# Attention's opening with head 0's scores and values ahead of head 1's maxima, later rotations, and conversions spread over more slots

## The chip, the cores and the metric

The kernel runs on one core of a Trainium2 chip. The metric is the device time of one execution in microseconds; the time before is 953.85 us, the median of three runs (952.25 to 954.91).

## The reference

Four batches of 8 heads of attention (576 positions, 64 dimensions) with rotary embedding of q and k, then a gated feed-forward block that mixes positions, then a low-rank mixing with a two-layer block. Cut to what matters here:

```python
q_rot, k_rot = rotate(q), rotate(k)
scores = q_rot @ k_rot.T / sqrt(64)
scores = scores - max(scores, axis=-1)
attn = exp(scores); attn = attn / (sum(attn, axis=-1) + 1e-9)
x = attn @ v                      # all heads side by side
x = x + gated(x) @ w_out          # gelu, norm, mixing of positions
u = x + (x.T @ U @ V).T
out = u + relu(u @ w_ch1) @ w_ch2
```

## The kernel before

The first phase is attention over 32 heads; the later phases are not touched. Each head is worked in five chunks of 128 positions (the fifth has 64), two halves of 288 columns each. The loop over t from -20 to 162 at the end of attention is the clock of the phase: t counts slots, and a slot is one chunk of one head, five to a head. In each slot TensorE gets one tile of scores (`scores`, tile st, L249), some tiles of maxima (`row_max`, tile sm, L220), and the values (`values`, tile pv, L276) of the chunk three slots back (LAG). Everything else is put in a table by `later(t, fn)` and issued at the end of its slot. The order on every engine is the order in which this loop issues; all engines are scheduled by hand here, and each works its own queue in order.

Precision is kept by splitting a number into a rounded high part and the low part that is left. For each head the kernel builds four stacks of 128 partitions: Q1 and K1 for the first product (high parts, and K's low part below), Q2 and K2 for the second (Q's low part, and one extra row). The extra row of Q2 holds the row maxima, the extra row of K2 is -1, so that the second product also subtracts the maximum. So scores of a head need that head's maxima for all 576 positions: five sm tiles, each reduced by VectorE (tile MX, L225), a transposition on TensorE and a row into Q2. For heads from 2 on the row goes through a 5x128 transpose (L223), a copy (L228) and a DMA on ScalarE's queue (L230); for head 0 `first_row` does it with five products with the identity (L236) and two copies (L237, L238).

The stacks: `load` brings raw q and k (tile raw, 576 KB) over SP's queue, `rope` rotates them in three operations (L148, L149, L150; head 0 on VectorE, head 1 on VectorE and GpSimd, the rest on GpSimd). Heads 0 to 2 are split by `first_stacks` on ScalarE and VectorE (copies L196 and L198, low parts L209 and L210). Later heads go the usual way in `stacks`: `high` is one copy on ScalarE (Q1, L162) and a DMA into K (L164); `low` is a subtraction on GpSimd (L167) and two DMAs (L168 into K1, L169 within Q1). SP issues all of these in order with the raw loads and the rest.

The slots of these steps are tables of numbers. A head from 5 on rotates 26, 25 and 23 slots ahead of its first scores, its high step stands 20 ahead and its low step 17 (LEAD); heads 2 to 4 have LEAD_IN, heads 0 and 1 FIRST. Maxima run up to 13 slots ahead of scores (AHEAD, RAMP): their tiles pass through the three PSUM buffers ss that scores use too, so each needs the reduction or the exponential (L252 on ScalarE) of an earlier one. The values of a head gather in the single buffer pv and are read out by ScalarE (L292).

Two more things stand in the slots. Weights come as 64-bit floats and are converted in chunks on ScalarE, VectorE (four operations, L73 to L76) and GpSimd (MATRIX, SMALL: first slot and distance of steps). From slot 100 the result of the first batch is split again (XH on ScalarE, XL on GpSimd, L426; ROWS). And IDLE places warm matmuls (L439) of a zero tile on TensorE at chosen points of the opening; their result is not used.

```python
upto = 0 if t < -9 else NC if t < MAX_1 else max(2 * NC, min(t + AHEAD + 1, 2 * NC + RAMP * (t - RAMP_FROM) // 10, NC * NH))
```

This line sets how many maxima tiles have been issued by slot t; head 1's five (upto from 5 to 10) go at slot -1, in front of the first scores at slot 0.

Of the kernel before, what the change touches and what calls it, by code (L numbers as in the profile page):

```python
# [53 lines left out]
def tile_kernel(ctx: ExitStack, tc: tile.TileContext, qk, vv, tabs, w_in, g_ln, wsgT, b_sg, w_out, u_r, v_r, w1, w2, out):  # L54
# [98 lines left out]
    def stacks(h, ticks):  # L153
# [16 lines left out]
        if h < len(BY_ACT):  # L170
            steps = rope(nc.gpsimd, h) + first_stacks(h)
        else:
            steps = rope(nc.gpsimd, h) + (high, low)
            if h < NS:
                steps += lambda: nc.gpsimd.memset(f(K2[D:]), -1.0),
            value_stacks(h)
# [11 lines left out]
    def first_stacks(h):
# [4 lines left out]

        def copy(on_act, out, x):
            if on_act:
                nc.scalar.activation(out, x, AF.Copy)  # L196
            else:
                nc.vector.tensor_copy(out, x)  # L198

        def high():  # L200
            e = BY_ACT[h]
            copy(e[0], K1[z], rot[z])
            copy(e[1], K1[a], rot[z])
            copy(e[2], Q1[a], rot[a])
            copy(e[3], Q1[z], rot[a])
            copy(e[4], K2[a], rot[z])

        def low():
            nc.vector.tensor_tensor(K1[z], rot[z], f(K1[z]), ALU.subtract)  # L209
            nc.vector.tensor_tensor(Q2[a, :S], rot[a], f(Q1[a]), ALU.subtract)  # L210
        value_stacks(h)
        return high, low
# [177 lines left out]
    for h in range(1, NR):  # L390
        load(h)
    for i in range(2):
        load_v(i)
    for i in range(len(BY_ACT)):
# [48 lines left out]
    for t in range(T0, NC * NH + LAG):  # L443
# [3 lines left out]
        if 0 <= t < NC * NH:  # L447
            if t < 3:
                warm(7 + t)
# [472 lines left out]
```

## Time and profile before

| | us |
|---|---|
| median of three runs | 953.85 |
| the profiled execution, its own time | 953.18 |
| its span, first to last instruction | 951.4 |
| attention, from the span's start to the next phase's first matmul | 304.95 |
| of it, from the start to the first scores | 32.34 |

| engine | busy, share of the span |
|---|---|
| PE, TensorE's matmuls | 97% |
| DVE, VectorE | 56% |
| ACT, ScalarE | 36% |
| POOL, GpSimd | 39% |

The profile names engines as in the second table; PEld is TensorE's loading of weights, SPq and ACTq are queues that issue DMAs. Shares over the whole span mix phases with different limits, so the stretches and the engines' rows in order of time are read for the phase that the change touches. A busy TensorE counts pipelined matmuls, and the warm matmuls too.

### The profile page before, as it was taken

How to read it: one execution, taken by the hardware profiler on the slowest of the kernel's cores; microseconds unless marked ns; L12 is line 12 of the kernel's file. 1: busy time of each engine (PE TensorE's matmuls, PEld its weight loads, DVE VectorE, ACT ScalarE, POOL GpSimd, SP SyncE). 2: the span in 40 equal slices, each digit the busy share in tenths (PEclk: the TensorE clock that was granted, in tenths of full speed). 3: DMA queues.
4: the chain of work that ended last, by engine and by line, in shares of the span. 5: the costliest groups of instructions: out<-in, count | busy, mean ns of one | idle time of the engine just before them, and what ended most of it. 6: DMA issues, size and time to landing. Idle time of an engine off the chain costs nothing.

```text
span 951.4 us, 13147 instructions
## 1 busy us (share of the span) xinstructions
PE 926.0 (97%) x5180; PEld 786.5 (83%) x5180; DVE 535.3 (56%) x720; ACT 345.6 (36%) x550; POOL 371.2 (39%) x289
## 2 busy tenths in 40 slices
PE   6899999999999998999999899999999999999998
PEld 2588888888877988999999787888888888888887
DVE  7797888887895496334248746642652552222222
ACT  4376656666665543314224323311320320101000
POOL 7788776877741765231427523200210220000000
PEclk7999999999999999999999999999999999999999
DMA  5579767676651500000003002220220210000112
GB/s 176 142 214 189 201 177 194 173 188 177 171 147 27 176 1 1 1 1 23 1 23 112 23 22 62 94 66 1 89 89 1 67 45 0 1 1 23 45 49 85
DMA packets 57300, 77.93 MB, mean 82 GB/s; under 512 B 29755, under 2 KB 33110, under 8 KB 57238
## 3 DMA queue, kind: packets, MB, share of 16 engines
q1 hardware_dynamic: 56928, 77.01, 29.3%
q8 instruction: 41, 0.67, 0.3%
q14 instruction: 21, 0.17, 0.1%
q10 hardware_dynamic: 310, 0.08, 0.0%
HBM read 55.02 MB, written 4.79 MB: 63 GB/s over the span
## 4 chain that ended last, share of the span: by engine, by line
PE 84%; DVE 9%; issue 2%; DMA 2%; POOL 2%; ACT 1%; SPq 0%; DVEq 0%; ACTq 0%; POOLq 0%
PE a L549 21%; PE r L549 20%; PE pv L276 14%; PE st L249 9%; PE w L549 5%; PE sm L220 4%; PE v L549 3%; PE m L549 3%; PE u L549 3%; DVE g L630 1%; DVE t L75 1%; DVE MX L225 1%; DVE t L73 1%; PE t L653 1%; DVE t L76 1%
## 5 line engine op out<-in xcount | busy, mean ns | idle before, releaser
L276 PE MATMUL pv<-pc,VV 128*65 128x288 f32 x512 | 144.7, 405 | 0.5 <-DVE sums L297 0.5
L225 DVE TENSOR_REDUCE MX<-sm 128x1 f32<-128x576 f32 (+1 forms) x160 | 119.1, 752 | 41.1 <-PE sm L220 37.7
L249 PE MATMUL st<-Q,K 65*128 65x288 f32 (+3 forms) x640 | 125.6, 319 | 0.3 <-DVE MX L225 0.3
L742 DVE SCALAR_TENSOR_TENSOR RL<-r,RH 128x1024 fp32r<-128x1024 f32 (+1 forms) x38 | 42.3, 1112 | 123.8 <-ACT RH L741 123.7
L741 ACT ACTIVATE RH<-r 128x1024 fp32r<-128x1024 f32 (+1 forms) x38 | 35.5, 936 | 207.2 <-PE r L549 207.2
L249 PEld LDWEIGHTS st<-Q,K 65*128 65x128 f32 (+3 forms) x640 | 95.9, 179 | 11.8 <-DVE MX L225 1.0
L757 DVE TENSOR_TENSOR X<-a,X 128x256 f32<-128x256 f32 (+4 forms) x65 | 46.4, 745 | 90.8 <-PE a L549 90.7
L252 ACT ACTIVATE pc<-st 128x576 f32<-128x576 f32 x128 | 82.6, 646 | 37.8 <-PE st L249 34.7
L549 PE MATMUL a<-RH,setB 128*128 128x512 f32 (+1 forms) x320 | 93.3, 368 | 0.0
L276 PEld LDWEIGHTS pv<-pc,VV 128*65 128x65 f32 x512 | 68.6, 136 | 29.5 <-DVE sums L297 0.7
L220 PE MATMUL sm<-K,Q 128*128 128x288 f32 (+1 forms) x320 | 76.5, 324 | 11.7 <-ACT K L196 5.8
L549 PE MATMUL a<-RH,setA 128*128 128x512 f32 (+1 forms) x288 | 83.5, 366 | 0.0
L549 PE MATMUL r<-UH,setB 128*128 128x512 f32 (+1 forms) x256 | 73.2, 363 | 0.0
L549 PE MATMUL r<-UH,setA 128*128 128x512 f32 (+1 forms) x256 | 72.9, 363 | 0.1
L220 PEld LDWEIGHTS sm<-K,Q 128*128 128x128 f32 (+1 forms) x320 | 52.3, 184 | 19.6 <-ACT K L196 8.3
L549 PEld LDWEIGHTS a<-RH,setB 128*128 128x128 f32 x320 | 58.2, 188 | 10.0
L513 POOL TENSOR_TENSOR setB<-t,setB 128x512 fp32r<-128x512 f32 x16 | 20.7, 1294 | 102.9 <-ACT setB L702 91.8
L549 PEld LDWEIGHTS a<-RH,setA 128*128 128x128 f32 x288 | 52.1, 188 | 9.2
L549 PE MATMUL a<-RL,setB 128*128 128x512 f32 (+1 forms) x160 | 58.9, 368 | 0.0
L167 POOL TENSOR_TENSOR Q<-raw,Q 128x576 fp32r<-128x576 f32 x29 | 43.0, 1483 | 34.0 <-ACT Q L162 33.9
L149 POOL TENSOR_TENSOR raw<-raw,tab 128x576 f32<-128x576 f32 x31 | 53.8, 1734 | 5.9 <-DMA raw<-in_qk 5.9
L549 PEld LDWEIGHTS r<-UH,setA 128*128 128x128 f32 x256 | 46.1, 188 | 8.4 <-DVE X L683 0.4
(170 smaller groups left out, 1968.4 us busy)
## 6 DMA issues: line engine op xcount, KB each, us to landing
raw<-in_qk SPq DMA_DIRECT2D x31, 576.0 KB
raw<-in_w SPq DMA_DIRECT2D x24, 512.0 KB
K<-Q SPq DMA_DIRECT2D x29, 288.0 KB
VV<-in_vv SPq DMA_DIRECT2D x16, 320.0 KB
rb<-rr SPq DMA_DIRECT2D x15, 288.0 KB
K<-Q SPq DMA_DIRECT2D x29, 144.0 KB
Q<-Q SPq DMA_DIRECT2D x29, 144.0 KB
raw<-in_w_in SPq DMA_DIRECT2D x8, 512.0 KB
```

What stands on the lines that cost most here:

```text
L149: lambda: e.tensor_tensor(raw[:, 1], raw[:, 1], tab[:, 1], ALU.mult),
L167: nc.gpsimd.tensor_tensor(Q2[:, :S], rot, f(Q1), ALU.subtract)
L220: nc.tensor.matmul(ps[:TS[t], n, :HALF], Q1[:, t * P:t * P + TS[t]], K1[:, n * HALF:(n + 1) * HALF], start=True, stop=True)
L225: nc.vector.tensor_reduce(MXs[h % 2][:TS[t], t:t + 1], ps[:TS[t], :, :HALF], AX.XY, ALU.max)
L249: nc.tensor.matmul(ps[:kk, n, :HALF], l[:, c * P:c * P + kk], r[:, ns], start=st, stop=not st)
L252: nc.scalar.activation(h2(pc[:kk]), ps[:kk, :, :HALF], AF.Exp, scale=0.125)
L276: nc.tensor.matmul(o, l, r, start=(c == 0 and j == 0), stop=(c == NC - 1 and j == len(pr) - 1))
L513: return nc.gpsimd.tensor_tensor(out, a, b, ALU.subtract)
L549: nc.tensor.matmul(o, l, rr, start=(j == 0), stop=(j == n - 1))
L741: nc.scalar.activation(RH[:, s], ps[:, :, :WIDE[blk]], AF.Relu)
L742: nc.vector.scalar_tensor_tensor(RL[:, s], ps[:, :, :WIDE[blk]], 0.0, f(RH[:, s]), ALU.max, ALU.subtract)
L757: nc.vector.tensor_tensor(X[b][:, e2, xs], ps[:, :n, us], X[b][:, e2, xs], ALU.add)
```

## The change

The opening is written anew. Head 0: `early_stacks` deals its copies and low parts to ScalarE and VectorE without going through slots; `first_head` issues its five maxima tiles with the row pieces in between, in the pv buffer. Then four scores tiles and three values tiles of head 0 come ahead of head 1's maxima, which are issued in slot 4 around the rest of the values; head 1's row is made the way of head 0's (`row_piece`, tile second_row). Head 1 is rotated on GpSimd alone, behind a memset that waits for one on VectorE, and that one stands behind head 0's low parts. Head 2 takes the usual way over GpSimd and DMAs. Of 39 warm matmuls 26 are left, all at the start.

From head 2 on the slots are: rotation at b, b + 2 and b + 3, high step at high_at(h), low step one slot later, where b is high_at(h - 1) and high_at(h) is the larger of 5h - 20 and 8 + 4.55(h - 4): the second up to head 20, equal or the first from then on. Heads 2 to 4 have numbers of their own (LEADS). Maxima follow `maxima(t)`, which starts 9 slots ahead of scores at slot 12 and comes to 13. SMALL and MATRIX move the conversions; the last five chunks stay at slots 130 to 150. XL's four operations move from slots 134 to 146 to slots 148 to 157. SP's first loads have the first values in front of head 3's raw data.

```diff
-LEAD = 26, 25, 23, 20, 17
-LEAD_IN = (-20, -19, -19, -8, -8), (-19, -18, -16, -3, -1, 4), (-3, -3, 0, 2, 4, 8)
-FIRST = (-17, -10), (-9, -9)
-LOAD, LOAD_V, SPLIT_V = 30, 7, (2, -1)
-AHEAD, RAMP_FROM, RAMP, MAX_1, ROW, ROW_0, ROW_1 = 12, -1, 25, -1, 2, -8, -9
+LEADS = {2: (-8, -8, -8, 3, 3), 3: (-7, 4, 4, 4, 5), 4: (4, 6, 7, 8, 9)}
+LOADS = {4: -6, 5: 3, 6: 5, 7: 7}
+MAXIMA = {5: 12, 6: 14, 7: 15, 8: 15, 9: 17, 10: 19, 11: 20}
+def high_at(h):
+    return max(5 * h - 20, 8 + 455 * (h - 4) // 100)
+def maxima(t):
+    return MAXIMA.get(t) or min(21 + (t - 12) * 25 // 23, t + 13)
+LOAD, LOAD_V, SPLIT_V = 35, 7, (2, -1)
+ROW = 1
-MATRIX = ((20, 1), (40, 10), (80, 10)) + tuple((t, 1) for t in range(130, 155, 5))
-SMALL, CONVERT, ROWS = ((5, 1), (10, 1), (15, 1)), 5, (100, 134)
-IDLE = 17, 2, 5, 0, 2, 5, 6, 1, 0, 1
+MATRIX = ((50, 10), (55, 10), (95, 10)) + tuple((t, 1) for t in range(130, 155, 5))
+SMALL, CONVERT, ROWS = ((5, 5), (25, 5), (90, 10)), 5, (100, 148)
+IDLE = 26
...
+    def early_stacks(h):
...
+        if h == 0:
+            return [act(K1[z], rot[z]), dve(K1[a], rot[z]), dve(Q1[a], rot[a]), act(Q1[z], rot[a])] + lows + [act(K2[a], rot[z])]
+        return [act(K1[a], rot[z]), act(Q1[a], rot[a]), dve(K1[z], rot[z])] + lows + [act(Q1[z], rot[a]), act(K2[a], rot[z])]
...
-            later(tick + 1, lambda: nc.scalar.dma_start(row, f(mt)))
+            if done > 5:
+                later(tick + 1, lambda: nc.scalar.dma_start(row, f(mt)))
+            else:
+                nc.scalar.dma_start(row, f(mt))
+    def row_piece(h, ps, t):
+        nc.tensor.matmul(ps[:1, t // 4, t % 4 * P:(t % 4 + 1) * P], MXs[h][:, t:t + 1], ident, start=True, stop=True)
...
+    def first_head():
+        ps = psp.tile([P, 2, 512], F32, tag="pv", name="first_row", bufs=1)
         for t in range(NC):
-            nc.tensor.matmul(ps[:1, t // 4, t % 4 * P:(t % 4 + 1) * P], MXs[0][:, t:t + 1], ident, start=True, stop=True)
-        nc.scalar.activation(Q2s[0][D:D + 1, :4 * P], ps[:1, 0, :4 * P], AF.Copy)
-        nc.vector.tensor_copy(Q2s[0][D:D + 1, 4 * P:], ps[:1, 1, :P])
+            row_max(0, t, None, 0)
+            if t > 1:
+                row_piece(0, ps, t - 2)
+        for t in (NC - 2, NC - 1):
+            row_piece(0, ps, t)
...
+    load(1)
+    load(2)
+    load_v(0)
+    load(3)
+    load_v(1)
...
+    for fn in rope(nc.vector, 0) + tuple(early_stacks(0)):
         fn()
...
+    nc.vector.memset(MXs[1], 0.0)
+    nc.gpsimd.memset(MXs[1], 0.0)
+    for fn in rope(nc.gpsimd, 1):
+        fn()
+    for tick, fn in zip((-8, -8, -8, -8, -8, 1, 3), early_stacks(1)):
+        later(tick, fn)
+    value_stacks(0)
...
     for h in range(2, NH):
-        stacks(h, LEAD_IN[h - 2] if h < 5 else [NC * h - o for o in LEAD])
+        b = high_at(h - 1)
+        stacks(h, LEADS.get(h) or (b, b + 2, b + 3, high_at(h), high_at(h) + 1))
     for h in range(NR, NH):
-        later(NC * h - LOAD - NC * (h > 2 * NR), lambda h=h: load(h))
+        later(LOADS.get(h) or max(NC * h - LOAD, high_at(h - NR) + 2), lambda h=h: load(h))
...
+        if t == -9:
+            first_head()
+        if t == NC:
+            values(0, 4, t)
+            ps = psp.tile([P, 2, 512], F32, tag="ss", name="second_row", bufs=3)
+            for c in range(NC):
+                row_piece(1, ps, c)
...
         if 0 <= t < NC * NH:
             scores(*divmod(t, NC))
+        if t == NC - 1:
+            for c in range(1, 3):
+                values(0, c, t)
+            for c in range(3):
+                row_max(1, c, None, t)
+            low_parts(len(lows))
+            values(0, 3, t)
+            for c in range(3, NC):
+                row_max(1, c, None, t)
-        upto = 0 if t < -9 else NC if t < MAX_1 else max(2 * NC, min(t + AHEAD + 1, 2 * NC + RAMP * (t - RAMP_FROM) // 10, NC * NH))
+        upto = 0 if t < NC else min(maxima(t), NC * NH)
...
-                    last[m] = t + ROW if m > 1 else ROW_1 if m else ROW_0
+                    last[m] = t + ROW + (m > 12)
...
+        if t == LAG:
+            values(0, 0, t)
```

On TensorE, where head 0's scores begin. Names: sm0_4 is the last maxima tile of head 0, sm1_4 that of head 1, st0_0 the first scores tile, pv0 the values of head 0, pc0_0 its exponentials; the last number only tells buffers apart. Before:

```order
L220 MATMUL sm1_4_288<-K_1_100,Q1_1_95 64x288 x2
L439 LDWEIGHTS idle_117
L439 MATMUL warm_296<-idle_117 128x512
L249 MATMUL st0_0_298<-Q1_0_94,K_0_99 128x288 x2
L249 MATMUL st0_0_298<-Q2_0_104,K_0_99 128x288 x2
L220 MATMUL sm2_0_305<-K_2_101,Q1_2_96 128x288 x2
L223 MATMUL sm2_0_305<-ident_61,MX_1_110 5x128
L220 MATMUL sm2_1_312<-K_2_101,Q1_2_96 128x288 x2
L249 MATMUL st0_1_320<-Q1_0_94,K_0_99 128x288 x2
L249 MATMUL st0_1_320<-Q2_0_104,K_0_99 128x288 x2
L220 MATMUL sm2_2_327<-K_2_101,Q1_2_96 128x288 x2
L220 MATMUL sm2_3_331<-K_2_101,Q1_2_96 128x288 x2
```

Now:

```order
L210 MATMUL sm0_4_223<-K_0_99,Q1_0_94 64x288 x2
L226 MATMUL first_row_204<-ident_61,MX_0_109 1x128 x3
L252 MATMUL st0_0_242<-Q1_0_94,K_0_99 128x288 x2
L252 MATMUL st0_0_242<-Q2_0_104,K_0_99 128x288 x2
L252 MATMUL st0_1_250<-Q1_0_94,K_0_99 128x288 x2
L252 MATMUL st0_1_250<-Q2_0_104,K_0_99 128x288 x2
L252 MATMUL st0_2_258<-Q1_0_94,K_0_99 128x288 x2
L252 MATMUL st0_2_258<-Q2_0_104,K_0_99 128x288 x2
L252 MATMUL st0_3_266<-Q1_0_94,K_0_99 128x288 x2
L252 MATMUL st0_3_266<-Q2_0_104,K_0_99 128x288 x2
L279 MATMUL pv0_273<-pc0_0_247,VV_0_111 65x288 x2
L252 MATMUL st0_4_284<-Q1_0_94,K_0_99 64x288 x2
```

The first scores stood behind head 1's last maxima tile and a warm matmul; now they stand behind head 0's own maxima and row pieces, with values of head 0 right after.

On VectorE, the same place. MX_0 and MX_1 are the maxima, K_0, Q1_0 and Q2_0 stacks of head 0, K_1 and so on of head 1. Before:

```order
L225 TENSOR_REDUCE MX_0_109<-sm0_0_199 128x1
L225 TENSOR_REDUCE MX_0_109<-sm0_1_203 128x1
L225 TENSOR_REDUCE MX_0_109<-sm0_2_207 128x1
L225 TENSOR_REDUCE MX_0_109<-sm0_3_211 128x1
L225 TENSOR_REDUCE MX_0_109<-sm0_4_215 64x1
L198 CAST Q1_1_95<-raw1_90 64x576
L209 TENSOR_TENSOR K_1_100<-raw1_90,K_1_100 64x576
L210 TENSOR_TENSOR Q2_1_105<-raw1_90,Q1_1_95 64x576
L238 CAST Q2_0_104<-first_row_229 1x128
L198 CAST K_2_101<-raw2_91 64x576
L209 TENSOR_TENSOR K_2_101<-raw2_91,K_2_101 64x576
L210 TENSOR_TENSOR Q2_2_106<-raw2_91,Q1_2_96 64x576
```

Now:

```order
L197 CAST K_0_99<-raw0_89 64x576
L197 CAST Q1_0_94<-raw0_89 64x576
L198 TENSOR_TENSOR K_0_99<-raw0_89,K_0_99 64x576
L198 TENSOR_TENSOR Q2_0_104<-raw0_89,Q1_0_94 64x576
L408 MEMSET MX_1_110 128x5
L215 TENSOR_REDUCE MX_0_109<-sm0_0_205 128x1
L215 TENSOR_REDUCE MX_0_109<-sm0_1_209 128x1
L215 TENSOR_REDUCE MX_0_109<-sm0_2_213 128x1
L215 TENSOR_REDUCE MX_0_109<-sm0_3_218 128x1
L215 TENSOR_REDUCE MX_0_109<-sm0_4_223 64x1
L232 CAST Q2_0_104<-first_row_204 1x128
L197 CAST K_1_100<-raw1_90 64x576
```

Head 2's three operations are gone from here, head 0's parts begin with a second cast, the memset of MX_1 stands behind the low parts, and the row's copy (CAST Q2_0) comes right behind head 0's maxima instead of behind head 1's parts.

On GpSimd, the beginning of the rotations. Before:

```order
L402 MEMSET VS_1_114 128x2
L149 TENSOR_TENSOR raw1_90<-raw1_90,tab_93 128x576
L150 TENSOR_TENSOR raw1_90<-raw1_90 128x576
L148 TENSOR_TENSOR raw2_91<-raw2_91,tab_93 128x576
L149 TENSOR_TENSOR raw2_91<-raw2_91,tab_93 128x576
L150 TENSOR_TENSOR raw2_91<-raw2_91 128x576
L148 TENSOR_TENSOR raw3_92<-raw3_92,tab_93 128x576
```

Now:

```order
L409 MEMSET MX_1_110 128x5
L155 TENSOR_TENSOR raw1_90<-raw1_90,tab_93 128x576
L156 TENSOR_TENSOR raw1_90<-raw1_90,tab_93 128x576
L157 TENSOR_TENSOR raw1_90<-raw1_90 128x576
L155 TENSOR_TENSOR raw2_91<-raw2_91,tab_93 128x576
L156 TENSOR_TENSOR raw2_91<-raw2_91,tab_93 128x576
L157 TENSOR_TENSOR raw2_91<-raw2_91 128x576
L155 TENSOR_TENSOR raw3_92<-raw3_92,tab_93 128x576
L189 TENSOR_TENSOR VS_0_113<-VV_0_111,VS_0_113 128x2x64
L174 TENSOR_TENSOR Q2_2_106<-raw2_91,Q1_2_96 128x576
```

Head 1's rotation has three operations here instead of two and stands behind the memset of MX_1, which waits for VectorE's; head 2's low part (Q2_2) has come in.

## Rows read from the trace of the kernel before

**Rows 1.** Stretches: length, busy PE, PEld, DVE, ACT, POOL; clock, DMA share, GB/s
```profile
0.00:25.00 25.00, 16.24 (x56) 7.54 (x57) 18.21 (x19) 10.83 (x16) 18.15 (x27) 0.80 0.57 170
50.00:75.00 25.00, 25.00 (x153) 20.34 (x151) 23.88 (x35) 17.88 (x34) 21.84 (x18) 1.00 0.80 211
```

**Rows 2.** Chain of waits: start, length, what, 52 to 56 us
```profile
52.34 1.50 PE pv L276 x8
53.84 0.53 PE st L249 x4
54.37 0.27 PE sm L220 x2
...
55.17 0.97 PE pv L276 x4
```

**Rows 3.** TensorE in order of time: start, length, engine, line, operation
```profile
1.17 6.45 PE L439 MATMUL warm<-idle 128*128 128x512 bf16 x17 [1.17 <-DVE idle L386]
13.44 1.78 PE L220 MATMUL sm<-K,Q 128*128 128x288 f32 x6 [5.82 <-ACT K L196]
...
32.34 1.52 PE L249 MATMUL st<-Q,K 128*128 128x288 f32 x4
...
45.19 0.69 PE L249 MATMUL st<-Q,K 128*128 128x288 f32 x4
```

**Rows 4.** VectorE in order of time
```profile
7.46 0.76 DVE L150 TENSOR_TENSOR raw<-raw 128x576 f32<-128x576 f32 x1
...
11.46 1.84 DVE L209 TENSOR_TENSOR K<-raw,K 64x576 fp32r<-64x576 f32 x1
...
15.10 3.40 DVE L225 TENSOR_REDUCE MX<-sm 128x1 f32<-128x576 f32 x5
...
23.38 0.28 DVE L238 CAST Q<-first_row 1x128 fp32r<-1x128 f32 x1
23.69 1.25 DVE L198 CAST K<-raw 64x576 fp32r<-64x576 f32 x1
...
28.60 2.73 DVE L225 TENSOR_REDUCE MX<-sm 128x1 f32<-128x576 f32 x4
```

**Rows 5.** GpSimd in order of time
```profile
12.64 1.93 POOL L148 TENSOR_TENSOR raw<-raw,tab 128x576 f32<-128x576 f32 x1
...
17.87 1.40 POOL L148 TENSOR_TENSOR raw<-raw,tab 128x576 f32<-128x576 f32 x1
```

**Rows 6.** ScalarE in order of time
```profile
8.25 0.68 ACT L196 ACTIVATE K<-raw 64x576 fp32r<-64x576 f32 x1 [6.25 <-DVE raw L150]
...
33.90 0.65 ACT L252 ACTIVATE pc<-st 128x576 f32<-128x576 f32 x1 [9.70 <-PE st L249]
```

**Rows 7.** SP's queue in order of time
```profile
24.03 0.67 SPq L164 DMA_DIRECT2D K<-Q  x1
...
30.35 0.47 SPq L169 DMA_DIRECT2D Q<-Q  x1
...
127.98 0.62 SPq L164 DMA_DIRECT2D K<-Q  x1
...
132.09 0.46 SPq L169 DMA_DIRECT2D Q<-Q  x1
```

**Rows 8.** Groups by line and shape, 40 to 280 us: busy us, mean ns | idle before
```profile
L149 POOL TENSOR_TENSOR raw<-raw,tab 128x576 f32<-128x576 f32 x26 | 45.3, 1743 | 0.0
L167 POOL TENSOR_TENSOR Q<-raw,Q 128x576 fp32r<-128x576 f32 x28 | 41.1, 1468 | 34.0 <-ACT Q L162 33.9
L150 POOL TENSOR_TENSOR raw<-raw 128x576 f32<-128x576 f32 x26 | 38.7, 1489 | 0.9
...
L260 DVE TENSOR_TENSOR ph<-pt,ph 64x576 fp32r<-64x576 f32 x28 | 26.3, 939 | 1.5
```

**Rows 9.** The same view as Rows 1, stretches of 2 us
```profile
10.00:12.00 2.00, 0.00 (x0) 0.00 (x0) 1.97 (x2) 1.02 (x2) 1.92 (x2) 0.50 1.21 298
...
24.00:26.00 2.00, 1.40 (x7) 0.48 (x6) 1.97 (x2) 0.20 (x2) 2.00 (x2) 1.00 0.72 170
```

More of the change, by code (lines that the diff above doesn't have):

```diff
@@ L169, in low @@
             nc.sync.dma_start(f(Q1[z]), f(Q1[a]))
[L170 to L176, printed above, removed]
+        steps = rope(nc.gpsimd, h) + (high, low)
+        value_stacks(h)
         for tick, fn in zip(ticks, steps):
@@ L192, in first_stacks @@
         a, z = slice(0, D), slice(D, P)
[L194 to L212, printed above, removed]
+        act = lambda out, x: lambda: nc.scalar.activation(out, x, AF.Copy)
+        dve = lambda out, x: lambda: nc.vector.tensor_copy(out, x)
+        low = lambda out, x, hi: lambda: nc.vector.tensor_tensor(out, x, f(hi), ALU.subtract)
+        lows = [low(K1[z], rot[z], K1[z]), low(Q2[a, :S], rot[a], Q1[a])]
+        if h == 0:
+            return [act(K1[z], rot[z]), dve(K1[a], rot[z]), dve(Q1[a], rot[a]), act(Q1[z], rot[a])] + lows + [act(K2[a], rot[z])]
+        return [act(K1[a], rot[z]), act(Q1[a], rot[a]), dve(K1[z], rot[z])] + lows + [act(Q1[z], rot[a]), act(K2[a], rot[z])]
     def row_max(h, t, done, tick):
@@ L389, in tile_kernel @@
         nc.sync.dma_start(RAW[0][:, x], qk[0, 0, x])
[L390 to L394, printed above, removed]
+    load(1)
[3 more added lines that the diff above has]
+    load_v(1)
+    for i in range(NS):
         nc.gpsimd.memset(f(K2s[i][D:]), -1.0)
@@ L397, in tile_kernel @@
         nc.gpsimd.memset(VVs[i][:, :, :, D:], 1.0)
-    for i in range(2):
-        nc.gpsimd.memset(MXs[i], 0.0)
+    nc.gpsimd.memset(MXs[0], 0.0)
     for i in range(2):
@@ L429, in tile_kernel, with low_parts @@
         later(ROWS[0] + 5 * k, lambda k=k: x_hi(0, k))
[L430 to L442 removed]
+        later(ROWS[1] + 3 * k, lambda k=k: x_lo(0, k))
+    ps = psp.tile([P, 2, 512], F32, tag="ss", name="warm", bufs=3)[:, 0]
+    for _ in range(IDLE):
+        nc.tensor.matmul(ps, idle[:, :P], idle, start=True, stop=True)
+    def low_parts(n):
+        for fn in lows[:n]:
+            fn()
+        del lows[:n]
+    n_max, last = 2 * NC, {}
     for t in range(T0, NC * NH + LAG):
         v = divmod(t - LAG, NC)
[L445 removed]
+        if t == -9:
[5 more added lines that the diff above has]
+                row_piece(1, ps, c)
+        if v[0] > 0 and v[1] == NC - 1:
             values(*v, t)
         if 0 <= t < NC * NH:
[L448 to L449 removed]
             scores(*divmod(t, NC))
[L451 to L455 removed]
+        if t == NC - 1:
[7 more added lines that the diff above has]
+                row_max(1, c, None, t)
+        low_parts(len(lows) - (0 <= t < NC * NH and t % NC in SPLITS))
+        if v[0] > 0 and v[1] == 0:
             values(*v, t)
[L457 removed]
+        upto = 0 if t < NC else min(maxima(t), NC * NH)
         ready = [m for m, due_at in last.items() if due_at <= t]
@@ L462, in tile_kernel @@
             last.pop(done, None)
-            if done == 0:
-                warm(1)
-                first_row()
-                continue
-            if m == 1:
-                warm(2 + c)
             row_max(m, c, done, t)
```

39 lines of the change are left out of this document (10 added, 29 removed).

## The prediction

> **What bounds the kernel now.** I read the table by stretches first. In the first 25 us TensorE is busy for 16.24 us, and much of that is filler; from 50 to 75 us it is busy for all 25.00 [rows 1]. The chain of waits then shows what fills it: scores, maxima and values follow each other with no wait between them [rows 2]. One tile of scores (st, four matmuls) costs 0.53 us, one of maxima (sm, two) 0.27, one of values (pv) 0.97, and the last values tile of a head 1.50 less 0.97 = 0.53. A head is 5 x 0.53 + 5 x 0.27 + 4 x 0.97 + 0.53 = 8.4 us, with one short transpose 8.5, and a slot (a fifth of a head) 1.70. So attention is TensorE's sum plus the time until it is full, and only that opening can be shortened by another order.
>
> The opening is read from each engine's rows in order of time. On TensorE, seventeen warm matmuls, maxima of head 0 from 13.44, but first scores at 32.34 [rows 3]. On VectorE the reason: head 0's low parts beside GpSimd take 1.84 each where a quiet 128x576 operation takes 0.76; its maxima are done at 18.50; then come the parts of heads 1 and 2, up to 28.6, and only then head 1's maxima [rows 4]. ScalarE has its first exponential at 33.90 [rows 6]. Head 0's row of maxima was complete at 23.66 [rows 4], nine microseconds before TensorE used it.
>
> **The change, part by part.** All times are of the profiled execution (953.18 us; the median of the runs is 953.85, 0.67 above it).
>
> Head 0's parts. VectorE's rotation ends at 8.22 [rows 4]. It now makes two casts, then both low parts, and GpSimd is held back by the memset behind them, so each low part costs 0.76 + 0.01 instead of 1.84. No row shows such a cast with GpSimd quiet. The bounds are 1.25 beside GpSimd [rows 4] and half of the 0.68 that the copy costs ScalarE [rows 6]; I take 0.68, as the same copy. 8.25 + 2 x 0.70 + 2 x 0.77 gives 11.2. (The Trainium skill, "VectorE: DVE Perf Modes", section "The perf-mode tier table", has fp32 copies at twice the pace of two-input operations, an estimate of 0.46 for this cast; by it everything below would be 0.4 us earlier. No run here shows it.) Five maxima at 0.68 [rows 4] end at 14.65, the last row piece (two short matmuls, under a maxima tile's 0.27) and its copy (0.28 [rows 4]) add 0.25 + 0.3 + 0.1: 15.3, and st0_0 is done at 15.6 instead of about 33.9.
>
> Head 1's rotation, all on GpSimd, starts at 11.25, now beside maxima only. Such an operation took 1.40 where VectorE was reducing and 1.93 beside low parts [rows 4, 5]: 3 x 1.40 gives 15.45. VectorE no longer does its first multiplication (0.76, hidden or not, it is in front of head 0's casts before).
>
> ScalarE then has two copies of head 1 ahead of the first exponential: 0.68 + 0.68 + 0.65 [rows 6] gives 17.5. That frees the buffer for st0_3. TensorE goes on: st0_3, pv0_0, st0_4, pv0_1, pv0_2, or 2 x 0.53 + 3 x 0.97 = 3.97, gives 21.5. Beside that VectorE makes head 1's parts, a cast of 1.25 and two low parts of 1.84 [rows 4], from 15.45 to 20.4: hidden by 1.1 us; were the cover gone, each further microsecond would count in full.
>
> Head 1's maxima: 0.27, five reductions of 0.68 and, in front of the fourth, the low part of head 0's last probabilities at 0.94 [rows 8]: 26.1. A row piece, two copies (512 values priced as a reduction, 128 at 0.28: 0.25 + 0.7 + 0.3) and half a scores tile (0.27): st1_0 is done at 27.7. The values of head 0 stand inside this and need nothing of their own.
>
> Then maxima of head 2, paced by reductions through three PSUM buffers: four reductions from 28.0 end at 30.7, then st1_3, pv1_0, a transpose, st1_4 (2.15): TensorE is at sm3_0 at 32.9. Head 3's stack must be there. GpSimd from 15.45: head 2's rotation beside low parts 1.93 + 1.93 + 1.40, head 3's first multiplication 1.40, the small value split 0.5 (an estimate, 128 of 576 columns), head 2's low part 1.5, two more of head 3 at 1.74 and 1.49 [rows 5, 8]: 27.4. ScalarE's copy, 0.68: 28.1. The K copy takes from issue to landing as long as the copy of Q behind it waits: 4.1 us (127.98 to 132.09), 6.3 in the crowded opening (24.03 to 30.35) [rows 7]. I take 4.1, since fewer raw loads stand beside it now: 32.2; the Q copy moves half the bytes and lands about 2 us later: 34.2. So sm3_0 starts at about 34, on the stack, and after it TensorE is full.
>
> The sum. At 45.19 TensorE before starts st1_2 [rows 3]. Counted in its order, it has then done 19 tiles of maxima, 7 of scores and head 0's values. The change at sm3_0 has done 15, 10, and one more values tile: -4 x 0.27 + 3 x 0.53 + 0.97 = +1.5 us, so before stood there at 46.7. Gain 46.7 - 34.0 = 12.7 us. Some ten hand-overs between engines lie on my path; one shows 13.30 to 13.44 on the way from VectorE's low part to the first maxima [rows 3, 4]. Part of them is in the pitches I used; 0.7 for the rest leaves 12.0. 953.2 - 12.0 = 941.2, on the scale of the median 941.8; I say **941.5**.
>
> What costs nothing. 13 warm matmuls less (39 to 26): they stood in waits. Head 2's parts go from VectorE to the usual way over GpSimd and DMAs, in the path above. Later rotations every 4.55 slots are 7.7 us per head; GpSimd needs 1.40 + 1.74 + 1.49 + 1.47 [rows 5, 8] and half a value split, 6.4. Conversions move to later slots on VectorE, which is at 23.88 of 25 in the worst stretch already without delaying TensorE [rows 1]. On SP the raw loads now stand behind one K and one Q copy, and the value load in front of head 3's raw load, 320 KB early. The four XL operations move to slots 148 to 157 of GpSimd, after the last rotation, and are first read after slot 162. From the last scores on the five engines have the same rows in both, so nothing later can eat a shift.
>
> **Rivals.**
>
> The clock stays low in the opening. The granted clock was 0.50 (1.2 GHz) at 10 to 12 us, after TensorE had stood idle since 7.62 [rows 3, 9]. The change has short pauses between reductions from 10 to 28. Against: at 24 to 26, busy for 1.40 of 2.00, the clock was 1.00 (2.4 GHz) [rows 9], and nine more warm matmuls now follow the seventeen that ended at 7.62. Price: TensorE's items on my path, 0.27 + 0.5 + 0.27 + 3.97 + 0.54 = 5.5 us, twice: 947. The Trainium skill, "TensorE: Matmul & The Clock Gate", section "A second HAM failure mode: psum-queue depth-cycling", speaks for this rival: micro-idles between matmul groups that cycle through PSUM make the clock swing; by that rule it would be 947, and rows 9 do not bear it out. Chance 0.10.
>
> GpSimd or a copy is late at heads 2 to 6. With 6.3 for the K copy of head 3, sm3_0 starts at 36.2; with every GpSimd operation at 1.93, 7.7 + 0.3 = 8.0 per head is over 7.7 and some lead is eaten: 2 to 4 us, 944. Chance 0.08.
>
> Slower: each head's stack arrives late. ScalarE's copy stands 5 slots (8.5 us) ahead of the head's first maximum for some 17 heads (4 to 20), where it stood 7 (11.9). From it: 0.68, K copy 4.1, issue 0.6, Q copy 2.0 = 7.4, which fits by 1.1. At 6.3 it is 9.6, late by 1.1 in each head: 941.5 + 17 x 1.1 = 960. It decides from a K copy of 5.9 us (0.7 x 17 = 12). For it: one row of 6.3, and SP now waits for GpSimd's low part with loads behind it. Against: that row fell in the crowded opening, and the low part stands 4 slots ahead of the maxima in both. Chance 0.10.
>
> No change: the opening is held by something I don't see, such as head 1's maxima taking back all. Since these stand on VectorE for 3.4 us only, chance 0.05, 953.
>
> **Numbers.** Forecast 0.67, so faster 0.67 + 0.10 + 0.08 = 0.85, same 0.05, slower 0.10; 0.3% (2.9 us) is about what a measurement can tell. Low end: casts at half (0.7), head 3's stack not in the way (34.0 to 32.9, 1.1), hand-overs at nothing (0.7), 0.5 for the runs' spread: 938.5. High end: the clock rival, 947. Outside lie the slower and the no-change cases and little else.
>
> **What would show it.** Right: first scores near 15 us and first exponential near 17; GpSimd's first multiplication not before VectorE's memset; first scores of head 1 near 27.7; TensorE full from about 34; attention's end, 304.95 before, near 293; all later stretches as long as before. Wrong: granted clock 0.50 between 14 and 28 (first rival); waits of maxima tiles for DMAs at heads 4 to 20 (slower); first scores early, but TensorE not full until after 38 (the second).

## The result and the profile after

The changed kernel takes 961.57 us (median of six runs, 958.64 to 963.72) against 953.76 (six runs, 952.25 to 954.91): ratio 1.0085, interval 1.0065 to 1.0105. It is slower by 7.8 us where 12 us less were forecast. The profiled execution took 961.14 us, its span is 959.4 (951.4 before). By TensorE's rows attention ends at 311.14 instead of 304.79, 6.35 later (304.95 is the same place in the chain of waits). The other 1.7 us fall after attention in this one execution (granted clock 0.90 in 350 to 375, 0.93 in that of before). In the traces of the experiments that part is 643.1 to 648.0 us long (646.6 before, 648.3 in the changed kernel), though no edit touches it; so the loss to be explained is the one in attention.

The stretches after, same columns as [rows 1]:

```profile
0.00:25.00 25.00, 20.84 (x92) 11.64 (x92) 16.05 (x22) 11.01 (x17) 16.82 (x29) 0.93 0.63 186
25.00:50.00 25.00, 21.60 (x124) 16.28 (x125) 16.66 (x25) 11.60 (x20) 19.65 (x15) 1.00 0.63 167
50.00:75.00 25.00, 22.45 (x125) 17.44 (x124) 12.75 (x21) 13.04 (x25) 15.93 (x12) 0.93 0.70 181
75.00:100.00 25.00, 23.56 (x141) 18.80 (x140) 17.27 (x27) 14.51 (x27) 20.30 (x17) 1.00 0.76 177
...
125.00:150.00 25.00, 21.23 (x109) 16.54 (x108) 14.53 (x20) 11.54 (x20) 13.43 (x11) 0.86 0.73 156
150.00:175.00 25.00, 24.20 (x147) 19.36 (x145) 18.57 (x27) 14.67 (x28) 19.90 (x14) 1.00 0.77 188
175.00:200.00 25.00, 25.00 (x153) 20.32 (x152) 20.57 (x30) 16.18 (x29) 23.70 (x17) 1.00 0.75 196
```

Before, TensorE was full from 50 us on; now it is full only from 175. Nor is another engine full in its place: from 25 to 175 VectorE, ScalarE and GpSimd all have spare time. That is what waits for transfers look like; the waits themselves are read below.

The opening itself came nearly as forecast. TensorE in order of time, answering to [rows 3], then VectorE, answering to [rows 4]:

```profile
11.00 1.43 PE L210 MATMUL sm<-K,Q 128*128 128x288 f32 x6 [2.37 <-DVE K L198]
...
16.14 2.79 PE L252 MATMUL st<-Q,K 128*128 128x288 f32 x16
...
21.99 1.27 PE L210 MATMUL sm<-K,Q 128*128 128x288 f32 x6
...
35.38 0.69 PE L210 MATMUL sm<-K,Q 128*128 128x288 f32 x4
```

```profile
9.15 0.46 DVE L197 CAST K<-raw 64x576 fp32r<-64x576 f32 x1
...
10.10 0.76 DVE L198 TENSOR_TENSOR K<-raw,K 64x576 fp32r<-64x576 f32 x1
...
24.79 1.81 DVE L263 TENSOR_TENSOR ph<-pt,ph 64x576 fp32r<-64x576 f32 x1
```

First scores came at 16.14 (forecast 15.3), head 1's maxima at 21.99 (21.5), head 3's at 35.38 (34).

Where the gain went is seen by following the heads. In TensorE's rows in order of time each head has one row of its last values (pv from ph); the table gives its start before, and how much earlier (-) or later it is in the changed kernel and in the runs told of below (us):

| head | before | changed | row later | 4.3 slots | K by ScalarE | half loads | old opening | chunks back |
|---|---|---|---|---|---|---|---|---|
| 1 | 52.94 | -11.36 | -10.18 | -11.56 | -9.12 | -11.41 | +0.32 | -8.85 |
| 3 | 69.93 | -5.88 | -8.20 | -9.92 | -8.24 | -10.00 | +4.96 | -4.40 |
| 7 | 103.88 | -2.99 | -5.00 | -4.97 | -5.21 | -7.27 | +11.54 | -0.70 |
| 10 | 129.33 | -1.76 | -2.70 | -3.03 | -3.98 | -6.03 | +12.78 | +0.63 |
| 11 | 137.82 | +5.62 | +4.08 | -1.60 | -3.39 | -5.46 | +13.37 | +1.21 |
| 16 | 180.24 | +6.76 | +5.06 | -1.60 | -2.98 | -5.46 | +13.85 | +1.72 |
| 25 | 256.62 | +6.75 | +5.06 | -1.60 | -2.98 | -5.46 | +13.86 | +1.71 |

At head 1 the change is 11.4 us ahead. From head 1 to head 16 it loses 18.1, 4.4 of them between heads 2 and 3 and 7.4 between heads 10 and 11; after that nothing moves up to head 25. What TensorE waited for from 28 to 330 us (us in total, times, longest):

```profile
PE sm L210 <- DMA Q<-Q: 8.4, 5, 3.7
PE st L252 <- DMA Q<-mt: 0.8, 1, 0.8
```

Maxima tiles wait for the last transfer of a head's stack: the third rival. Two places show how. First the chain of waits from 43 to 55 us (heads 4 and 5):

```profile
43.24 0.50 PE sm L210 x2
43.75 0.12 PE sm L213
...
44.57 0.28 DVE mt L218
...
44.87 0.69 ACTq L223
...
45.66 0.69 ACT Q L169
...
46.42 1.41 POOL Q L174
47.83 1.39 POOL raw L156
...
49.24 1.42 SPq L175
...
50.75 4.03 DMA Q<-Q
...
54.91 0.51 PE sm L210 x2
```

This is a ring, a chain of waits that comes back to where it began. Head 4's first maxima tile (43.24) carries the transpose of head 3's maxima (L213); ScalarE issues that row's DMA (L223), for which it waits for VectorE's copy (mt); behind it in ScalarE's queue stands head 5's high copy (L169); then GpSimd's low part, SP's issues and the Q copy (4.0 us), and head 5's first maxima tile at 54.91. One turn takes 54.91 - 43.24 = 11.7 us, where a head is worth 8.5. The second place, 125 to 135 us (head 14), in the same view:

```profile
125.20 7.38 DMA K<-Q
...
132.59 2.32 DMA Q<-Q
...
135.06 0.82 PE sm L210 x2
```

Here the K copy took 7.4 us. ScalarE's high copy ahead of it, then SP's rows:

```profile
121.68 0.68 ACT L169 ACTIVATE Q<-raw 128x576 fp32r<-128x576 f32 x1
```

```profile
120.59 0.44 SPq L145 DMA_DIRECT2D raw<-in_qk  x1
121.08 0.46 SPq L350 DMA_DIRECT2D raw<-in_w_in  x1
122.67 0.47 SPq L324 DMA_DIRECT2D rb<-rr  x1
123.18 1.24 SPq L310 DMA_DIRECT2D rc<-stage  x2
124.52 0.59 SPq L149 DMA_DIRECT2D VV<-in_vv  x1
125.20 0.71 SPq L171 DMA_DIRECT2D K<-Q  x1
```

Two things add up. ScalarE's copy ended at 122.36, but SP works its queue in order and came to the K copy at 125.20, 2.8 us later, behind rb, two stage issues and a value load. And four transfers of 576, 512, 288 and 320 KB had been issued in the 4.6 us before it. From a K copy's issue to that of the Q copy behind it, which waits for it, it took 3.2 to 3.5 us at heads 2, 3, 4 and 6, where no load had been issued in the 2.5 us before, 3.7 at head 7 (one of 288 KB) and 4.2 to 7.4 at heads 8 to 15, where one or two loads had. (At head 5 the Q copy came right behind the low copy, L175, the DMA of the low part into K1, which SP held up; so its 4.4 us are no length of a K copy.) How much of head 14's wait of 3.7 us belongs to SP's order and how much to the length of the copy, no run separates.

Each long wait costs a second time. Stretches of 2 us behind the two waits (columns as above, granted clock third from the right):

```profile
54.00:56.00 2.00, 1.08 (x8) 1.06 (x9) 0.43 (x1) 0.00 (x0) 0.00 (x0) 0.95 0.51 171
56.00:58.00 2.00, 2.00 (x6) 1.11 (x5) 0.51 (x2) 0.66 (x2) 0.00 (x0) 0.50 0.02 5
58.00:60.00 2.00, 2.00 (x10) 1.53 (x9) 1.25 (x4) 1.32 (x5) 1.90 (x2) 0.69 0.33 71
...
136.00:138.00 2.00, 2.00 (x8) 1.53 (x7) 1.77 (x4) 1.10 (x2) 2.00 (x2) 0.50 1.04 325
```

After each of the two waits the clock is 0.50 (1.2 GHz) for a while: an estimate from the stretches between 54 and 60 is 0.1 + 1.0 + 0.6 = 1.7 us, and about 3 between 135 and 142 (0.58, 0.50, 0.50 and 0.71 in the stretches from 134).

### The profile page after: what moved, and what is told of

It reads as the page before. It is cut to its first block, busy times and chain, and to the rows that moved or that the text cites. A ratio compares the mean times of both kernels' runs of the same rounds, so it can differ in the third digit from the quotient of the medians.

```text
span 959.4 us, 13099 instructions
## 1 busy us (share of the span) xinstructions
PE 929.9 (97%) x5176; PEld 787.6 (82%) x5176; DVE 520.2 (54%) x718; ACT 341.8 (36%) x546; POOL 376.6 (39%) x292
## 4 chain that ended last, share of the span: by engine, by line
PE 78%; DVE 8%; DMA 5%; issue 3%; POOL 3%; ACT 2%; SPq 0%; ACTq 0%; POOLq 0%; DVEq 0%
PE a L561 21%; PE r L561 20%; PE pv L279 12%; PE st L252 7%; PE w L561 5%; PE sm L210 3%; PE m L561 3%; PE u L561 3%; PE v L561 3%; DMA K<-Q 2%; DMA Q<-Q 2%; DVE g L642 1%; DVE t L82 1%; DVE MX L215 1%; DVE t L80 1%
## 5 line engine op out<-in xcount | busy, mean ns | idle before, releaser
L279 PE MATMUL pv<-pc,VV 128*65 128x288 f32 x512 | 146.7, 410 | 0.5 <-DVE sums L300 0.5
L255 ACT ACTIVATE pc<-st 128x576 f32<-128x576 f32 x128 | 82.3, 645 | 38.9 <-PE st L252 32.9
L210 PE MATMUL sm<-K,Q 128*128 128x288 f32 (+1 forms) x320 | 76.1, 326 | 11.4 <-DMA Q<-Q 8.4
L561 PE MATMUL a<-RL,setA 128*128 128x512 f32 (+1 forms) x144 | 52.8, 367 | 0.0
```

What stands on the lines that cost most here:

```text
L210: nc.tensor.matmul(ps[:TS[t], n, :HALF], Q1[:, t * P:t * P + TS[t]], K1[:, n * HALF:(n + 1) * HALF], start=True, stop=True)
L255: nc.scalar.activation(h2(pc[:kk]), ps[:kk, :, :HALF], AF.Exp, scale=0.125)
L279: nc.tensor.matmul(o, l, r, start=(c == 0 and j == 0), stop=(c == NC - 1 and j == len(pr) - 1))
L561: nc.tensor.matmul(o, l, rr, start=(j == 0), stop=(j == n - 1))
```

## The experiments

All but the one called old opening are the changed kernel with the edit named, and each is timed beside the kernel before in the same runs. "The row edit" is the first of them.

**Row later.** The row DMAs of heads 3 to 5 go behind the high copy.

```diff
-            if done > 5:
+            if done > 2:
                 later(tick + 1, lambda: nc.scalar.dma_start(row, f(mt)))
```

> Edit: the row DMAs of heads 3 to 5 go one slot later on ScalarE's queue, behind the high copy of two heads on instead of in front of it. In the changed kernel the high copy of head 5 stood behind head 3's row DMA, which waits for a transpose that rides on head 4's first maxima tile, so it waited for head 4's stack (copy at 45.66 after an idle of 1.96 us, head 5's first maxima at 54.91 after 2.35). Theory (a ring: stack, maxima, row, next copy, next stack): the copy of head 5 moves to 43 to 44 us, that of head 6 to 52 or earlier, TensorE's wait near 52 to 55 goes, the clock stays 1.00 in 50 to 75, and the median falls by 3 to 6 us to 956 to 958.5. Rival (only the transfers are slow, the order on ScalarE doesn't matter): first maxima of head 5 still 2 us late, 961.5 within 1.

Measured 956.32 us, ratio 1.0037 (1.0018 to 1.0056), so 4.6 us less than the changed kernel's 1.0085. ScalarE's rows now have the copy of head 5 first:

```profile
44.79 0.68 ACT L169 ACTIVATE Q<-raw 128x576 fp32r<-128x576 f32 x1
...
46.02 0.69 ACTq L221 DMA_DIRECT2D Q<-mt  x1
```

Head 5's maxima waited 0.56 us instead of 2.35, and the clock from 50 to 75 was 1.00. The ring is shown. What it was worth is less sure: 4.6 us by the two medians (2 to 7 with their intervals); in the two traces the changed kernel loses 5.5 us from head 1 to head 3 and this one 2.0, but at head 25 it is only 1.7 us ahead. The expectation was off in detail: the copies came at 44.8 and 54.3, not 43 to 44 and 52. The wait at head 14 stayed (3.43).

**Loads behind.** Raw loads from head 8 on right behind a K copy instead of ahead of the next.

```diff
-        later(LOADS.get(h) or max(NC * h - LOAD, high_at(h - NR) + 2), lambda h=h: load(h))
+        later(LOADS.get(h) or max(NC * h - LOAD, high_at(h - NR + 1)), lambda h=h: load(h))
```

> Edit: the raw loads from head 8 on are issued right behind the K copy of a head instead of between the Q copy of one head and the K copy of the next. Theory (the K copy is long because 576 KB of raw data and more are queued in front of it: 6.3 us at 89.17 and 7.4 at 125.20 against 3.2 at 37.59): K copies of heads 10 and 14 fall to 3 to 5 us, their waits of 1.3 and 3.7 us shrink or go, the clock in 125 to 150 rises from 0.86 towards 1.00, median 953 to 957. Rival (the length comes from the share of the DMA engines whatever the order, or from the other loads): K copies as long as before, 961.5 within 1.5; a raw load behind the K copy may also delay the Q copy, up to 964.

Measured 963.11 us, ratio 1.0116 (1.0081 to 1.0151): no gain. Two K copies did become short (3.3 us at heads 9 and 10, where 4.6 and 6.3 stood), others didn't (5.3 at head 8, 4.7 and 6.1 at heads 12 and 13). Scores now waited for rows, whose DMA of 2.5 KB took 4.1 to 4.9 us beside the load, and the ring at head 5, inside which head 8's load now stands on SP's queue, got longer (a wait of 3.2 us). The delay was handed on to another transfer, as the expectation's last clause feared for the Q copy.

**Lead of 10.** Maxima not more than 10 slots ahead of scores.

```diff
-    return MAXIMA.get(t) or min(21 + (t - 12) * 25 // 23, t + 13)
+    return MAXIMA.get(t) or min(21 + (t - 12) * 25 // 23, t + 10)
```

> Edit: maxima stop at 10 slots ahead of scores instead of going on to 13, so from head 7 on the distance between the high copy and the head's first maxima tile grows from 5 slots to 6 at head 10, 7 at head 12, 8 at head 15 and 10 from head 20. Nothing else moves. Theory (stack late because of 5 slots): heads 4 and 5 stall as in the changed kernel (2 to 3 us and a low clock in 50 to 75), heads 10, 14 and 16 don't; from 100 us on TensorE is full, median 952 to 955. Rival (a slow K copy would stall at any lead, or the loss has another source): 960 to 963. Second rival (rows now late: the last maxima tile stands 5 slots ahead of the scores that need its row): waits of scores tiles for the row's DMA, 965 or more.

Measured 989.02 us, ratio 1.0388 (1.0357 to 1.0419), the second rival. What TensorE waited for:

```profile
PE st L252 <- DMA Q<-mt: 18.9, 13, 3.4
...
PE sm L210 <- DMA Q<-Q: 3.7, 3, 2.2
```

The stacks gained by it (3.7 us instead of 8.4), the rows lost far more, at heads all through attention. So 10 slots are too few for the row, and the lead of stacks can't be taken from the lead of maxima by that much; 11 and 12 weren't tried.

**All three** edits together:

> Edit: the three edits of the runs before it together. Theory (all of the loss is stacks that arrive late at heads 4 to 16): the gains add up where they are of different heads (row later: heads 5 and 6; lead 10: from head 10 on), TensorE is full from about 50 us on, attention ends near 297 to 301 instead of 311, median 945 to 951, so faster than the kernel before. Rival (the opening's shift is eaten by something after attention or by the clock): attention ends earlier but the median stays over 953.

Measured 988.17 us, ratio 1.0394 (1.0356 to 1.0432): the rows' waits outweigh what the other two edits bring, so the sum of the gains couldn't be seen and the theory's number is missed.

**4 slots and 4.3 slots.** The row edit, and rotations and high copies in quicker succession.

```diff
-    return max(5 * h - 20, 8 + 455 * (h - 4) // 100)
+    return max(5 * h - 20, 8 + 4 * (h - 4))
...
```

> Edit, on top of the later row DMAs of heads 3 to 5: rotation and high copy every 4 slots instead of 4.55 until they reach 5h - 20 (at head 12 instead of head 20), so the high copy stands 6 slots ahead of the head's first maxima at head 7 and 8 at head 10, where it stood 5. Maxima and rows stay. Theory (the high copy is too near to the maxima): the waits of 1.5 us at head 10, 0.4 and 0.6 at heads 12 and 13, and 3.4 at head 14 go, with the pause on the buffers at 129 and the low clock in 125 to 150; TensorE is full from about 56 us on; 956.3 less 8 us of idle time between 75 and 175 and 1 to 2 of low clock gives 945 to 948, faster than the kernel before. Rival (GpSimd can't rotate every 6.8 us beside the value splits and conversions, at 5.7 to 6.4 us of work per head): ScalarE waits for rotations with exponentials behind it, TensorE waits for buffers, 954 or more.

> As the run before it with 4.3 slots instead of 4: high copy 5 slots ahead of the first maxima at heads 5 to 8, 6 at heads 10 to 12, 8 from head 14 or 15. Theory (stack late because of the distance): between the two, head 10 still late by some tenths, head 14 not; 947 to 951. If GpSimd is the limit at 4 slots, this one is the better of the two, 946 to 950.

Measured 952.64 us, ratio 1.0001 (0.9971 to 1.0031), and 952.39, ratio 1.0001 (0.9984 to 1.0018): 3 to 4 us below the row edit alone, level with the kernel before, and short of both expectations. Waits for stacks are gone as the theory said (0.4 and 0.6 us in all), and no wait for GpSimd came in their place, so the rival wasn't it. With 4 slots the executions lie far apart (946.1 to 957.7), and the profiled one took 955.6, 3 us over the median: its trace shows where time can go, and somewhat more of it than usual. The next wait is the row's; TensorE with 4 slots:

```profile
PE st L252 <- DMA Q<-mt: 7.5, 4, 3.9
...
PE sm L210 <- DMA Q<-Q: 0.4, 1, 0.4
```

and in the chain of waits, for the worst of them:

```profile
93.25 7.00 DMA Q<-mt
...
100.30 0.56 PE st L252 x2
```

Seven microseconds for 2.5 KB, beside a raw load, a K copy and the low copy into K, issued from 91.37 to 92.78. From 75 to 100 us the DMA share is 0.88.

**Old opening.** The kernel before, with the slots of the changed one from head 5 on and the changed maxima, rows and raw loads.

```diff
-        stacks(h, LEAD_IN[h - 2] if h < 5 else [NC * h - o for o in LEAD])
+        b = high_at(h - 1)
+        stacks(h, LEAD_IN[h - 2] if h < 5 else (b, b + 2, b + 3, high_at(h), high_at(h) + 1))
...
-        upto = 0 if t < -9 else NC if t < MAX_1 else max(2 * NC, min(t + AHEAD + 1, 2 * NC + RAMP * (t - RAMP_FROM) // 10, NC * NH))
+        upto = 0 if t < -9 else NC if t < MAX_1 else max(2 * NC, min(maxima(t), NC * NH))
```

> The kernel before with its own opening (heads 0 to 4, warm matmuls, first scores at 32 us, conversions as they were) and the changed kernel's slots from head 5 on: rotations every 4.55 slots, maxima 9 and later 13 slots ahead, row DMAs and raw loads as there. Theory (the loss is in the new slots alone): TensorE, which is full from 50 us in the kernel before, waits for stacks at heads 5 to 16 with low clock behind it, attention ends 8 to 17 us later than 304.95, median 960 to 970. Rival (the loss comes from the new opening, for instance from GpSimd or the loads being behind when slot 5 comes sooner): 951 to 956.

Measured 968.29 us, ratio 1.0154 (1.0125 to 1.0183), inside the theory's range. The table's last but one column says it: level at head 1, then 13.5 us lost by head 16. The opening gains 11.4, and the slots with the maxima, rows and raw loads that go with them lose that and more, even behind the old opening. So the loss doesn't need the new opening. Whether the new opening keeps its gain with the old slots, no run shows.

**K on ScalarE's queue.** The row edit, and the K copy issued by ScalarE.

```diff
-            nc.sync.dma_start(both, f(Q1[z]).rearrange("p (a s) -> p a s", a=1).to_broadcast([D, 2, S]))
+            nc.scalar.dma_start(both, f(Q1[z]).rearrange("p (a s) -> p a s", a=1).to_broadcast([D, 2, S]))
```

> Edit, on top of the later row DMAs of heads 3 to 5: the K copy is issued on ScalarE's queue, right behind the high copy, instead of SP's, where raw, value and reciprocal loads are queued in front of it. Theory A (it is long because it stands behind those loads in SP's order and ring): its time from issue to landing is 3.2 to 3.6 us everywhere, heads 10 and 14 are on time, 950 to 953. Theory B (it is long because loads in flight share the DMA engines, whatever the queue): as long as before where loads are in flight, 5 to 7 us, 955 to 958. In both ScalarE pays 0.6 to 1.3 us per head for the issue, with exponentials behind it, which may cost up to 3 us in all.

Measured 961.46 us, ratio 1.0084 (1.0054 to 1.0113). The K copy of head 10 is issued at 89.59, SP's Q copy behind it at 97.09, with SP's loads issued at 87.60 and 89.38:

```profile
87.60 0.46 SPq L324 DMA_DIRECT2D rb<-rr  x1
...
89.38 0.60 SPq L149 DMA_DIRECT2D VV<-in_vv  x1
...
97.09 0.49 SPq L176 DMA_DIRECT2D Q<-Q  x1
```

That is 7.5 us on another queue than the loads'; 3.3 at head 4, where no load had been issued for four microseconds. So theory B's mechanism is borne out: the length goes with the loads in flight, whatever the queue. The time itself is over both theories' ranges: it is 4 to 5 us above the row edit alone, where up to 3 were set down for ScalarE's issues, and which wait makes the rest isn't shown. (The Trainium skill, "DMA: Bandwidth & Descriptors", section "Queues, rings and completion order", has that the queues of SP and ScalarE run on the same sixteen engines; this run agrees. It also has these engines take turns between queues packet by packet. By that one might expect a 2.5 KB row to pass early; the row of 7.0 us above did not, and no run here says why.)

**Half loads.** The 4 slots, with the second half of each raw load of heads 4 to 17 left out. The rotations of these heads then work on old data in that half, with the same instructions: this kernel is a probe, not a candidate.

```diff
...
+            nc.sync.dma_start(RAW[h % NR][:, 0], qk[h // NHEAD, h % NHEAD, 0])
```

> The run with rotations every 4 slots again, with half of each raw load of heads 4 to 17 left out (288 KB instead of 576; the second plane keeps old data, so their rotation is of wrong numbers and the same instructions). Theory (what still delays rows and copies is the share of the DMA engines: 1.4 MB per head in 6.8 us): K copies fall from 6.3 to 7.8 us at heads 8 to 11 to 3.3 to 5, the row DMA that took 7.0 us takes 2 to 3, the four waits of scores tiles for rows (7.5 us) shrink to under 2, median 943 to 947. Rival (rows are late for their place on ScalarE's queue and the slot of their transpose, not for the DMA engines): waits of scores for rows stay over 5 us, 950 to 954.

Measured 947.25 us, ratio 0.9953 (0.994 to 0.9965), 5 us below the run with 4 slots and 0.25 above the theory's range. K copies of heads 8 to 11 took 4.5, 3.6, 4.4 (at most, the Q copy waited for the low copy) and 4.0 us instead of 6.5, 6.3, 7.4 and 7.8, and TensorE's waits for rows and stacks are nearly gone:

```profile
PE st L255 <- DMA Q<-mt: 0.4, 1, 0.4
...
PE sm L213 <- DMA Q<-Q: 0.2, 1, 0.2
```

So it is the raw loads in flight that delay both. (Half the load is half the bytes and half the pieces; which of the two counts, the run doesn't tell.)

**K by ScalarE.** The row edit, and for heads 4 to 13 ScalarE writes K's upper halves, with no K copy; then the same with 4.3 slots.

```diff
...
+            if h in BY_ACT:
+                nc.scalar.activation(K1[a], rot[z], AF.Copy)
+                later(ticks[3] + 1, lambda: nc.scalar.activation(K2[a], rot[z], AF.Copy))
+                return
...
```

> Edit, on top of the later row DMAs of heads 3 to 5, with the changed kernel's 4.55 slots: for heads 4 to 13 ScalarE writes K's two upper halves itself (two copies of 64x576, 0.68 us each, one with the high copy, one a slot later), and the K copy of 288 KB falls away. Theory (K copy and crowded DMA engines are the loss): the stack of a head comes 3 to 6 us sooner and the other transfers are less crowded; no wait for a Q copy at heads 5 to 13, head 14 (a K copy again) perhaps; 956 less 5 to 9: 947 to 951. Rival (ScalarE's 1.36 us per head delays exponentials, and scores wait for buffers): 954 or more.

> The same with rotations every 4.3 slots. Theory: with 4.3 slots alone no tile waited for a stack by more than 0.4 us, but scores for rows by 4.1 us and VectorE by 1; without the K copies of heads 4 to 13 the rows land sooner as well, 944 to 949, faster than the kernel before. Rival (rows late for their place in the order): as the run with 4.3 slots, 951 to 953.

Measured 949.06 us, ratio 0.997 (0.9957 to 0.9983), and 950.22, ratio 0.9984 (0.9966 to 1.0001). The first is inside the theory's range and faster than both kernels (0.003 x 953 = 2.9 us and, with the changed kernel's ratio, 11). No wait for a stack of 0.3 us or more is left; the row of head 7 (5.3 us, issued beside a raw load) still holds scores for 1.5. The share of the DMA engines from 60 to 90 us is 0.62 (0.75 in the changed kernel). The quicker succession brought nothing on top: its scores waited 4.8 us for rows, so its theory failed.

**Chunks back.** The conversions' slots as before, nothing else.

```diff
-MATRIX = ((50, 10), (55, 10), (95, 10)) + tuple((t, 1) for t in range(130, 155, 5))
-SMALL, CONVERT, ROWS = ((5, 5), (25, 5), (90, 10)), 5, (100, 148)
+MATRIX = ((20, 1), (40, 10), (80, 10)) + tuple((t, 1) for t in range(130, 155, 5))
+SMALL, CONVERT, ROWS = ((5, 1), (10, 1), (15, 1)), 5, (100, 148)
```

> The changed kernel with one part undone: the six conversions of the first hundred slots go back to the slots and step distances they had before (5, 10, 15, 20, 40, 80 instead of 5, 25, 90, 50, 55, 95); everything else as in the changed kernel. Theory (while the leads are being built up, heads 2 to 13, VectorE and the DMA engines have little to spare): 0.7 MB of weights and two conversions more fall between 30 and 75 us, so heads 2 to 8 lose more than the 8.4 us they lose in the changed kernel, by 2 to 6, and heads 9 to 13 lose less, since two loads of 512 KB are gone from 110 to 125; the sum 958 to 966, on either side of the changed kernel's. Rival (conversions are beside the point, as the prediction had it: nothing for the move): every head's loss within 1 us of the changed kernel's, 960 to 962.

Measured 958.32 us, ratio 1.0081 (1.0042 to 1.012): as the changed kernel within the interval. In the one trace (955.12 us, the fastest of its five runs) the loss from head 1 to head 8 is 8.2 us, as large as in the changed kernel (8.4) and not larger by 2 to 6; 2.5 us are lost ahead of it, and from head 8 to 16 it loses 2.4 instead of 9.7, since head 14's stack is in time: its K copy took 4.9 us instead of 7.4, with no weight load of 512 KB left around it, and SP came to it 1.1 us behind ScalarE's copy instead of 2.8. So the theory's first half and the rival fail, its second half (heads 9 to 13 lose less) holds in this trace, and whether the move is worth anything in sum stays open.

## Why the prediction was wrong

**Head 0 and the opening: right, with small errors.** The casts took 0.46 and 0.45, not 0.68. (The Trainium skill's "VectorE: DVE Perf Modes", section "The perf-mode tier table", by which the estimate was 0.46, is borne out.) Against that the rotation ended at 9.12 instead of 8.22, since raw data landed later, and head 0's last probabilities cost VectorE 1.81 instead of 0.94, with GpSimd busy beside it. Head 3's maxima came at 35.38, 1.4 late. The forecast had them wait for the stack; instead TensorE's own work, priced to reach that place at 32.9, filled the time up to them. At head 1 the change stood 11.4 us ahead, less 1.1 for four maxima tiles still to be made up: 10.3, where 12.0 was forecast.

**"After it TensorE is full": the step that failed.** It was full at 175, not 34, and lost 18.1 us on the way. The trace gives some 10.2 us of idle time from 36 to 180, 4.7 of low clock after the two long waits and 1.1 of postponed maxima; the remaining 2 are not placed. The sentence rested on the belief that the later slots of the stacks cost nothing, and on a K copy of 4.1 us "since fewer raw loads stand beside it now". From head 8 to 15 it took 4.2 to 7.4.

**The third rival was the case, but it got 0.10.** Its price (960; 961.57 measured) was near by luck: it had some 17 heads late by 1.1 us each, while five heads waited, 0.2 to 3.7 us and 8.4 in all, and low clock did much of the rest. Two readings kept its chance small. The first is the K copy of 4.1 us [rows 7]. For the kernel before it was fair. What SP waited for from 36 to 180 us, before:

```profile
SPq L169 <- DMA K<-Q: 6.2, 5, 1.8
```

and in the changed kernel:

```profile
SPq L176 <- DMA K<-Q: 39.7, 14, 5.1
```

Before, the Q copy waited for the K copy five times, and these K copies took 3.2 to 4.1 us. The longer rows of that trace, such as this one of 6.8 us, are something else:

```profile
102.53 0.62 SPq L164 DMA_DIRECT2D K<-Q  x1
103.20 0.59 SPq L138 DMA_DIRECT2D raw<-in_qk  x1
106.02 0.46 SPq L321 DMA_DIRECT2D rb<-rr  x1
...
108.50 0.76 SPq L168 DMA_DIRECT2D K<-Q  x1
109.35 0.55 SPq L169 DMA_DIRECT2D Q<-Q  x1
```

The Q copy follows 0.1 us behind the low copy (here L168), which had stood behind rb and others in SP's order; when the K copy landed, these rows don't show. Seven slots hid such waits, five don't. The rows also show what the change turned round: before, the raw load goes out 0.7 us behind the K copy; now it stands ahead of the next one, often with a second load beside it, and the K copies are longer. At heads 10, 14 and 15 they took 6.3, 7.4 and 6.0, over the 5.9 from which the rival decided; at head 3, for which the 4.1 was used, 3.5. The second reading is ScalarE's order: what stands in front of the high copy was never listed, so the ring wasn't seen.

The other rivals: the clock was 0.50 from 12 to 14 us and 0.79 from 14 to 16, after an idle time of 2.4 us, but 1.00 from 16 to 54, so the first rival came for head 0's maxima alone, and first scores were 0.8 late in all; later the clock fell after the waits. The second (2 to 4 us at heads 2 to 6) was right for head 5 alone. Of "what costs nothing" the traces show no wait for XL or for GpSimd's pace; the later rotations did cost, not GpSimd's time but the lead they took from the transfers, and the moved conversions put two loads of 512 KB in front of head 14.

What stays open: even with half the loads the gain at the end is 5.5 to 6 us, not 10; most of the rest goes at heads 3 to 11, up to 1.2 us at one of them, where TensorE's idle time from 36 to 180 us sums to 2.4 and no wait for a transfer is over 0.4. Not tried were the new opening with the old slots, and SP's order around head 14.

## What to carry to other kernels

Where steady work hides transfers, a lead that looks unused may be what hides them: before moving it later, ask from which head on each transfer is early enough again, and with how many bytes per microsecond until then. Price a transfer by rows in which it was the last thing waited for; a row that another wait ended is only a bound. Ask too whether the change puts loads in front of it. List what stands in front of each of its steps on every in-order queue: two chains that feed each other through one queue can close into a ring. A wait that is taken away shows the next one: here stack, then row, then the loads in flight.
